# R read by rows, W and R loaded singly, more transposes by DMA, and a new hand-made order in a fused recurrence and feed-forward kernel

## The chip, the cores and the metric

The kernel runs on one core of one Trainium2 chip. The metric is the time of the device for one execution, in microseconds (us). A core has a matrix engine (PE in the profile, with its weight loads as PEld), a vector engine (DVE), a scalar or activation engine (ACT), a general one (POOL), a queue engine that here only issues transfers (SP), and 16 DMA engines that carry the transfers. Each engine works through its own list of instructions in the order in which the program holds it, and waits where an operand isn't ready.

## The reference, cut to what matters

Inputs r, k, v, w, a, b have the shape [4 batches, 8 heads, 768 tokens, 40]. The state of a head is a 40x40 matrix.

```python
for t in range(S):
    y[:, :, t] = np.einsum('bhd,bhde->bhe', rt, state)
    Sa = np.einsum('bhde,bhe->bhd', state, at)
    state_decay = state * wt[:, :, None, :] - np.einsum('bhd,bhe->bhde', Sa, bt)
    state = state_decay + np.einsum('bhd,bhe->bhde', vt, kt)

x = y.transpose(0, 2, 1, 3).reshape(3072, 320)     # one row per token
h = np.maximum(x @ w_in, 0.0)                      # 320 -> 2048
out = (h * h) @ w_out                              # 2048 -> 320
```

## The kernel before

**Tiling.** The 768 tokens are cut into 6 chunks of 128. One chunk of one batch entry is called a batch here, m = 0 to 23; m // 4 is the chunk. A batch holds 128 tokens (on the partitions) of 8 heads; each head's 40 columns are padded to 64, so that two heads make 128 columns. Inside a chunk the recurrence is done by matrix products and masks, and a state (UZ) goes from chunk to chunk. A batch is two steps, st = 2m and 2m + 1, of four heads each: 48 steps.

**Preparation of a batch** (add_prep). Six loads (W, K, B, A, V, R) on the SP queue. ln(W) on ACT, split into a high and a low part (hi, lo), summed along the tokens by PE (cs, L333), and turned into decays by ACT (GI and GA, L357, E). KB, AA, V and R are products or casts in bf16. Then they are turned, tokens to columns: KBT, AT, VT, RT. "Turned" means either PE transposes into a PSUM bank (turn, L417) with a copy out by DVE (L240) or ACT (L237), or one DMA transpose on the SP queue (across, L446). Before the change KB is turned by DMA from batch 8 on, and A, V and R always by PE. R of the first four batches is loaded "by rows" (L305, two transfers, runs of 1280 bytes, eight tokens to a partition) and turned by 16 transposes of 64x64 (L513), and by four of 128x128 (L417) after that.

**The last decay** GL of each batch, the last token's row of GA turned to a column: four products with one column on PE and a DVE product with a mask (L376, L381) in the first six batches; later one DMA transpose for two batches (gD, L385) and a POOL or DVE product with the mask.

**A step** (add_step): ca (PE, L563), its mask (CN, two of 128x512 on DVE, L571), P, two corrections, Sn; then tb, ex (PE, L641), its mask (EVX, two of 128x512 on DVE, L646), y (PE, L661 to L675), Xn (DVE, L681), and the carried state UZ. **The feed-forward** (add_ff) takes one batch at a time for the first four and two at a time later: the result Xn of two steps gets its last 64 columns doubled ("dup"), is turned by PE (tx, L816) and copied (XT), goes through w_in (hr, L841, and hp, L854), relu (hs), square (Gt) and w_out (op, L888), and is stored (L896).

**Loads.** From batch 4 on one transfer brings two batches (L297, 320 KB); each of the six tensors has three such buffers.

**Order.** Nothing is scheduled by the compiler. ORDER is a string of numbers, the one list in which all operations are emitted, and so each engine's own order; WAYS says which engine does an operation that several can do (a copy, a product); BANKS which PSUM bank a product uses; IDLE adds products without use (L1060) ahead of a PE operation. A transfer that waits on SP holds all transfers behind it. On PE, "R" operations (ca, ex, hr, and R's 64x64 transposes) use the array in row halves, "F" operations all of it.

Of the kernel before, what the change touches and what calls it, by code (L numbers as in the profile page):

```python
# [7 lines left out]
FP32 = mybir.dt.float32  # L8
# [11 lines left out]
def kernel(  # L20
# [39 lines left out]
    RING = {"N": 3, "NW": 2, "lnW": 2, "GI": 2, "KB": 5, "GA": 2, "E": 3, "AA": 2, "V": 5, "R": 3, "SN": 8,  # L60
            "EVX": 3, "RT": 4, "VT": 4, "KBT": 3, "AT": 3, "GL": 4, "GD": 2, "CN": 3, "c1": 2, "x1": 2,
# [3 lines left out]
    SPLIT, THREE, ROWS, GLD, PAIR = 1, 6, 4, 6, 4  # L65
# [116 lines left out]
    def blank(ring, i):  # L182
# [6 lines left out]
        if ring == "KB":  # L189
            nc.vector.memset(t_[:, :, :, D:64], 0.0)  # L190
        elif ring in ("AA", "V", "R"):
            nc.vector.memset(t_[:, :, D:64], 0.0)
        elif ring == "GA":
            nc.vector.memset(t_[:, :, :, D:64], 0.0)
        elif ring == "SN":
            nc.gpsimd.memset(t_[:, :, D:64], 0.0)
        elif ring == "UZ":
            nc.vector.memset(t_[:], 0.0)
# [7 lines left out]
    for i in range(2):  # L206
        blank("SN", i)
# [3 lines left out]
    for ring, a_, b_, eng, cost, lat, r0 in (  # L211
            ("KB", 1, RING["KB"], "DVE", 0.145, 0.22, -1.5), ("V", 1, RING["V"], "DVE", 0.09, 0.17, -1.2),
            ("R", 1, RING["R"], "DVE", 0.09, 0.17, -1.2),
            ("AA", 1, 2, "DVE", 0.09, 0.17, -1.5), ("GA", 1, 2, "DVE", 0.09, 0.17, -1.0),
            ("SN", 2, RING["SN"], "POOL", 0.1, 0.2, -1.5), ("HM", 0, 1, "POOL", 0.16, 0.26, 2.0),
            ("UZ", 0, 2, "DVE", 0.9, 1.0, 0.5)):
        for i in range(a_, b_):
            rank = i + r0 if ring != "UZ" else (7.0, 0.5)[i]
            later[ring, i] = ("blank", ring, i)
            op(("blank", ring, i), eng, rank, cost, lat, [], [],  # L220
               lambda ring=ring, i=i: blank(ring, i))
# [11 lines left out]
    BY_DMA = {"KB": range(8, NBC), "V": (), "A": ()}  # L233
# [23 lines left out]
    for m in range(NBC):  # L257
        o = Batch()
        bt.append(o)
        o.nat = bt[m - 1].nat if m % 2 else {key: buf(f"N{key}") for key in "WKBAVR"}  # L260
        o.lnW, o.hi, o.lo, o.GI, o.KB, o.AA, o.V, o.R, o.VT, o.RT, o.KBT, o.AT, o.GL, o.Xn = (
            buf(x) for x in ("lnW", "hi", "lo", "GI", "KB", "AA", "V", "R", "VT", "RT", "KBT", "AT", "GL", "Xn"))
        o.GA, o.E, o.GD = (bt[m - 1].GA, bt[m - 1].E, bt[m - 1].GD) if m % 2 else (buf(x) for x in ("GA", "E", "GD"))
# [20 lines left out]
    def add_load(m, key, rank):  # L284
        o = bt[m]
        c, bb = divmod(m, NB)

        def tile_():
            return sb(o.nat[key], [128, 2, NHH, D], FP32)
# [879 lines left out]
```

## Time and profile before

| what | value |
|---|---|
| median of 3 runs | 257.37 us (256.85 to 257.81) |
| the profiled execution's own time | 256.97 us |
| its span in the trace | 255.4 us |
| DMA: hardware queue, software queue | 76.5%, 6.2% of 16 engines' span |
| DMA packets | 172256, of which 165047 under 512 B |

The rows in the prediction come from the first page, from answers that group instructions ("line engine op out<-in xcount | busy, mean ns"), from windows of the span (busy time of each engine in a stretch), from the timeline (start, duration, engine, line), and from lists of waits. Matrix products overlap in the pipeline, and the ends that the profile shows for them are modelled: their pace is read from one start to the next.

### The profile page before, as it was taken

The page shows a single profiled execution, that of the slowest core. Times are in us where ns is not written, and L with a number is a line of the kernel's source. Part 1 is how long each engine was busy: PE and PEld are TensorE (multiplying, and loading weights), DVE is VectorE, ACT ScalarE, POOL GpSimd, SP SyncE. Part 2 cuts the span into 40 slices and gives each one's busy share as a digit, 9 for nine tenths or more (in the row PEclk, how much of TensorE's full clock was granted, in tenths as well). Part 3 has the DMA queues.
Part 4 walks back from the last instruction along what each step waited for, and adds up shares of the span by engine and source line. Part 5 has one row for each costly group of instructions (what it writes and reads, how often), then busy time and mean ns, then how long its engine had stood idle before and what let it go on. Part 6 is the DMA issues. An engine that isn't in the chain of part 4 may idle for free.

```text
span 255.4 us, 9993 instructions
## 1 busy us (share of the span) xinstructions
PE 242.0 (95%) x3948; PEld 193.1 (76%) x3948; DVE 230.4 (90%) x556; ACT 215.6 (84%) x589; POOL 172.0 (67%) x259
## 2 busy tenths in 40 slices
PE   7978889999999999999999999999999999999993
PEld 7656667787787687887788777877788787878772
DVE  6799999998799999999999999999998898999482
ACT  3669978898698898899999999998999798877660
POOL 4366784886696969875568979995748694716340
PEclk9999999999999999999999999999999999999999
DMA  6999999999599979889988899988898989300111
GB/s 111 189 176 149 174 217 177 147 153 215 101 150 192 168 134 181 173 153 165 200 159 165 160 190 173 167 176 156 154 168 123 214 188 152 70 30 5 68 35 68
DMA packets 172256, 37.95 MB, mean 149 GB/s; under 512 B 165047, under 2 KB 170679, under 8 KB 172206
## 3 DMA queue, kind: packets, MB, share of 16 engines
q1 hardware_dynamic: 169646, 34.66, 76.5%
q0 software_dynamic: 2560, 2.62, 6.2%
q8 instruction: 31, 0.51, 0.9%
q14 instruction: 19, 0.16, 0.2%
HBM read 28.84 MB, written 3.93 MB: 128 GB/s over the span
## 4 chain that ended last, share of the span: by engine, by line
PE 51%; ACT 2%; DVE 2%; DMA 2%; issue 1%; POOL 0%; SPq 0%; POOLq 0%; DVEq 0%
PE bank L888 16%; PE bank L854 10%; PE bank L417 4%; PE bank L641 3%; PE bank L841 3%; PE bank L563 3%; PE bank L595 2%; PE bank L661 2%; DMA NA<-in_a_dram 2%; PE bank L333 1%; PE bank L669 1%; PE bank L623 1%; PE bank L816 1%; PE bank L586 1%; PE bank L628 1%
## 5 line engine op out<-in xcount | busy, mean ns | idle before, releaser
L646 DVE TENSOR_TENSOR EVX<-bank,MEX 128x512 bf16<-128x512 f32 x96 | 62.4, 683 | 1.6 <-PE bank L641 1.1
L571 DVE TENSOR_TENSOR CN<-bank,MCN 128x512 bf16<-128x512 f32 x96 | 61.3, 682 | 1.9 <-PE bank L563 1.0
L888 PE MATMUL bank<-WOUT,Gt 128*128 128x320 bf16 x384 | 59.4, 300 | 0.4 <-DMA WOUT<-in_moe_w_out_dram 0.4
L872 POOL TENSOR_TENSOR Gt<-hs 128x512 bf16<-128x512 bf16 x43 | 45.2, 1055 | 19.2 <-ACT hs L861 14.0
L854 PE MATMUL bank<-XT,WIN 128*128 128x256 bf16 (+1 forms) x448 | 54.5, 258 | 0.0
L861 ACT ACTIVATE hs<-bank 128x512 bf16<-128x512 f32 x77 | 45.5, 601 | 6.0 <-issue 2.5
L888 PEld LDWEIGHTS <-Gt 128*128 128x128 bf16 x384 | 35.4, 97 | 13.3 <-issue 0.8
L854 PEld LDWEIGHTS <-WIN 128*128 128x128 bf16 x448 | 34.8, 97 | 7.1 <-issue 3.6
L612 ACT ACTIVATE junk<-CN 128x512 bf16<-128x512 bf16 x48 | 30.6, 638 | 0.2
L341 POOL TENSOR_TENSOR lo<-hi 128x320 f16<-128x320 f32 x21 | 15.1, 720 | 15.0 <-ACT hi L237 8.5
L401 POOL TENSOR_TENSOR KB<-NB,GI 128x320 bf16<-128x320 f32 (+1 forms) x22 | 18.7, 854 | 8.3 <-ACT GI L357 6.8
L870 ACT ACTIVATE Gt<-hs 128x512 bf16<-128x512 bf16 x37 | 23.1, 636 | 1.4 <-DVE hs L863 1.4
L595 PEld LDWEIGHTS <-CN 128*128 128x128 bf16 x384 | 18.5, 96 | 5.3 <-issue 2.6
L401 POOL TENSOR_TENSOR KB<-NK,GI 128x320 bf16<-128x320 f32 x21 | 18.6, 888 | 5.5 <-ACT GI L357 5.5
L407 POOL TENSOR_TENSOR AA<-NA,E 128x320 bf16<-128x320 f32 x19 | 15.3, 809 | 10.1 <-DMA NA<-in_a_dram 7.5
L563 PE MATMUL bank<-AT,KBT 64*128 64x128 bf16 x384 | 18.0, 218 | 2.2 <-ACT KBT L237 0.7
L841 PE MATMUL bank<-XT,WIN 64*128 64x256 bf16 (+1 forms) x224 | 18.5, 256 | 0.0
L661 PE MATMUL bank<-KB,EVX 128*128 128x40 bf16 x384 | 17.2, 180 | 0.0
L563 PEld LDWEIGHTS <-KBT 64*128 64x128 bf16 x384 | 12.2, 94 | 6.6 <-issue 2.8
L750 POOL TENSOR_TENSOR x<-Mc,c 128x640 bf16<-128x640 bf16 x10 | 14.0, 1398 | 3.9 <-PE bank L641 3.8
L237 ACT ACTIVATE SNall<-bank 128x160 bf16<-128x160 f32 x38 | 11.4, 307 | 6.0 <-PE bank L595 4.5
L681 DVE TENSOR_TENSOR Xn<-bank,E 128x160 bf16<-128x160 f32 x48 | 14.7, 316 | 1.8 <-PE bank L669 0.7
(134 smaller groups left out, 652.6 us busy)
## 6 DMA issues: line engine op xcount, KB each, us to landing
out_dram<-osb SPq DMA_DIRECT2D x24, 160.0 KB, 2.4
NW<-in_w_dram SPq DMA_DIRECT2D x10, 320.0 KB, 4.5
NK<-in_k_dram SPq DMA_DIRECT2D x10, 320.0 KB, 5.5
NB<-in_b_dram SPq DMA_DIRECT2D x10, 320.0 KB, 5.1
NA<-in_a_dram SPq DMA_DIRECT2D x10, 320.0 KB, 5.2
NV<-in_v_dram SPq DMA_DIRECT2D x10, 320.0 KB, 5.3
NR<-in_r_dram SPq DMA_DIRECT2D x10, 320.0 KB, 4.9
E<-GA SPq DMA_DIRECT2D x9, 224.0 KB, 4.6
```

The lines of the kernel that those rows point to most:

```text
L401: engine(eng).tensor_tensor(out=o.KB.tile[:, u, h, 0:D], in0=o.nat[key].tile[:, m % 2, h], op=ALU.mult, in1=o.GI.tile[:, h])
L563: nc.tensor.matmul(out=quads(ca[s])[:, i, u, :], lhsT=o.KBT.tile[half(s), u, j0 + i, :], rhs=o.AT.tile[half(s), j0 + i, :], start=(i == 0 ...
L571: nc.vector.tensor_tensor(out=t_[:, :, s], in0=quads(ca[s]), in1=MCN[:], op=ALU.mult)
L595: nc.tensor.matmul(out=P[:, 2 * i + s], lhsT=CN[:, i, s, 1, :], rhs=X[:, 2 * i + s], start=False, stop=last, skip_group_check=True)
L612: nc.scalar.activation(out=t_, in_=CN_.tile[:, :, :, 1, :], func=ACTF.Square, accum_out=ACC[:, AN + st:AN + st + 1])
L646: nc.vector.tensor_tensor(out=sb(EV_, [128, 2, 2, 2, L], BF16)[:, :, s], in0=quads(ex[s]), op=ALU.mult, in1=MEX[:].rearrange("p (i u) x -> ...
L841: nc.tensor.matmul(out=hv(w_)[:, u], lhsT=WIN[2][half(w_), j * 128:(j + 1) * 128], rhs=XT()[half(w_), 2, 0:nb, :], start=(u == 0), stop=False,
L854: nc.tensor.matmul(out=hv(w_)[:, u], lhsT=WIN[g][:, (j0 + u) * 128:(j0 + u + 1) * 128], rhs=XT()[:, g, 0:nb, :], start=False, stop=(g == 1 ...
L861: nc.scalar.activation(out=t_, in_=hpb.tile[:], func=ACTF.Relu)
L870: nc.scalar.activation(out=t_, in_=x_, func=ACTF.Square)
L872: engine(eng).tensor_tensor(out=t_, in0=x_, in1=x_, op=ALU.mult)
L888: nc.tensor.matmul(out=opb.tile[:, 0:DM], lhsT=Gtb[h].tile[:, j, b_, :], rhs=WOUT[:, j, :], start=(j == 0), stop=(j == NJ - 1))
```

## The change

1. R of every batch is loaded by rows (runs of 1280 bytes, two transfers) and turned on PE by 16 transposes of 64x64. Before this held for batches 0 to 3.
2. W and R are loaded one batch at a time, in rings of five single buffers (K, B, A and V still two batches at a time).
3. The last decay GL comes from PE products in all 24 batches, and its mask product is on DVE; the nine DMA transposes gD are gone.
4. x is turned by DMA from batch 12 on, V from batch 14 on and A from batch 20 on: 12 + 10 + 4 transfers of 384, 512 and 512 columns. Their PE transposes and copies out of PSUM are gone.
5. At the start, only the pad columns of UZ are set to zero (768 of 2048 elements), and each such clearing may be on DVE or POOL.
6. ORDER, WAYS and BANKS are new; IDLE holds 42 products in place of 84.

```diff
-    SPLIT, THREE, ROWS, GLD, PAIR = 1, 6, 4, 6, 4
+    SPLIT, THREE, PAIR = 1, 6, 4
...
+        if ring == "UZ":
+            t_ = t_[:].rearrange("p i (s d) -> p i s d", s=2)
+        fill.memset(t_[..., D:64], 0.0)
...
-    BY_DMA = {"KB": range(8, NBC), "V": (), "A": ()}
+    BY_DMA = {"KB": range(8, NBC), "V": range(14, NBC), "A": range(20, NBC), "X": range(12, NBC)}
...
-        o.nat = bt[m - 1].nat if m % 2 else {key: buf(f"N{key}") for key in "WKBAVR"}
+        o.nat = dict(bt[m - 1].nat) if m % 2 else {key: buf(f"N{key}") for key in "KBAV"}
+        o.nat.update({key: buf(f"N{key}") for key in "WR"})
...
         op(("L", m, key), "SP", rank, 0.6, 0.6, [], [o.nat[key]],
-           two if m >= PAIR else rows if key == "R" and m < ROWS else go)
+           rows if key == "R" else pair if two else go)
...
-        def gl_row():
-            nc.sync.dma_start_transpose(out=sb(o.GD, [128, 2 * PB, 32], BF16)[:],
-                                        in_=o.GA.tile[96:128].rearrange("p b h e -> p (b h e)"))
-        if m < GLD:
...
+        op(("gl", m), "PE", s0 - 0.5, *pe(0.102), [("GA", m), ("GI", m)], [o.GA, csb], gl_mm, "F")
+        op(("GL", m), "DVE", s0 - 0.3, 0.075, 0.16, [("gl", m)] + cleared("HM", 0), [csb, o.GL], gl_ev)
...
         def t_r():
-            if m >= ROWS:
-                turn(bank(b4), [flat(o.R.tile[:, 2 * j:2 * j + 2, :]) for j in range(PB)])
-                return
             for i in range(8):
...
+                def across_x(b_=b_, Xn_=Xn_):
+                    nc.sync.dma_start_transpose(out=XT()[:, :, b_, :], in_=Xn_.tile[:, 0:NG * 128])
...
+                op(("XT", h, b_), "SP", 2 * m + 6.0, 1.25, 1.25, [("Xn", 2 * m), ("dup", h, b_)], [Xn_, X_], across_x)
...
-    IDLE = ((135, 29, 7), (42, 8, 1), (44, 23, 2), (90, 10, 0), (329, 6, 0), (929, 8, 5),)
+    IDLE = ((32, 14, 7), (60, 5, 1), (56, 6, 2), (65, 7, 0), (145, 5, 3), (106, 5, 3),)
```

What the new order does at three places. The rows are the instructions of one engine in its order.

**DVE at the start**, before the first mask (CN). Before, from the fourth clearing of a pad on:

```order
L192 MEMSET V_104 128x8x12
L198 MEMSET UZ_110 128x1024
L192 MEMSET R_108 128x8x12
L194 MEMSET GA_96 128x16x12
L242 TENSOR_SCALAR hi_188<-lnW_178 128x320
L192 MEMSET AA_101 128x8x12
L240 CAST R_107<-NR_169 128x8x40
L192 MEMSET R_109 128x8x12
L242 TENSOR_SCALAR hi_195<-lnW_184 128x320
L190 MEMSET KB_91 128x16x12
L192 MEMSET V_105 128x8x12
L192 MEMSET V_103 128x8x12
```

And now, at the same place:

```order
L192 MEMSET V_106 128x8x12
L238 TENSOR_SCALAR hi_184<-lnW_180 128x320
L192 MEMSET SNall 128x4x12
L238 TENSOR_SCALAR hi_211<-lnW_207 128x320
L192 MEMSET R_108 128x8x12
L388 TENSOR_TENSOR KB_90<-NB_170,GI_224 128x4x40
L340 TENSOR_TENSOR lo_230<-hi_211 128x320
```

Most clearings, the cast of R and the first lo have gone to POOL, and hi follows one clearing of a small pad. POOL's list there, between its last mask and its first lo:

```order
L192 MEMSET SNall 128x4x24 x2
L192 MEMSET KB_92 128x16x24
L192 MEMSET SNall 128x4x24
L192 MEMSET GA_96 128x16x24
L192 MEMSET UZ_110 128x32x24
L340 TENSOR_TENSOR lo_189<-hi_184 128x320
```

Before, POOL had only three clearings of SNall there, and the first lo was on DVE.

**SP near batches 20 to 22** (L434 is the DMA transpose of KB, V and A in the changed file, L304 a load of R by rows, L297 one for two batches). Before:

```order
L367 DMA E_98<-GA_95 15x1024
L446 DMA_TRANSPOSE KBT_618<-KB_90 128x8x128
L297 DMA NV_485<-in_v_dram 128x16x40
L446 DMA_TRANSPOSE KBT_333<-KB_91 128x8x128
L896 DMA out_dram<-osb_1600 128x320
L896 DMA out_dram<-osb_1848 128x320
L297 DMA NR_573<-in_r_dram 128x16x40
```

And now:

```order
L887 DMA out_dram<-osb_1876 128x320
L292 DMA NW_325<-in_w_dram 128x8x40
L434 DMA_TRANSPOSE AT_581<-AA_100 128x4x128
L434 DMA_TRANSPOSE AT_279<-AA_101 128x4x128
L434 DMA_TRANSPOSE KBT_271<-KB_91 128x8x128
L434 DMA_TRANSPOSE VT_876<-V_106 128x4x128
L297 DMA NK_595<-in_k_dram 128x16x40
L434 DMA_TRANSPOSE VT_354<-V_102 128x4x128
L304 DMA NR_219<-in_r_dram 64x1x320 x2
```

Transposes of A and V have come in between, and every one of them waits for a product or cast on POOL, DVE or ACT, with the loads behind it.

**SP at the end.** Before, from the last transpose of KB on:

```order
L446 DMA_TRANSPOSE KBT_618<-KB_93 128x8x128
L896 DMA out_dram<-osb_1696 128x320
L896 DMA out_dram<-osb_1848 128x320 x2
L896 DMA out_dram<-osb_1600 128x320
L896 DMA out_dram<-osb_1696 128x320
L385 DMA_TRANSPOSE GD_2130<-GA_95 128x8x32
```

And now, from the same one on:

```order
L434 DMA_TRANSPOSE KBT_579<-KB_93 128x8x128
L796 DMA_TRANSPOSE XT_830<-Xn_623 128x3x128
L796 DMA_TRANSPOSE XT_830<-Xn_973 128x3x128
L887 DMA out_dram<-osb_1876 128x320
L887 DMA out_dram<-osb_1607 128x320
L887 DMA out_dram<-osb_1779 128x320
L434 DMA_TRANSPOSE VT_769<-V_104 128x4x128
L304 DMA NR_709<-in_r_dram 64x1x320 x2
L887 DMA out_dram<-osb_1876 128x320
L434 DMA_TRANSPOSE VT_876<-V_105 128x4x128
L887 DMA out_dram<-osb_1607 128x320
L796 DMA_TRANSPOSE XT_923<-Xn_878 128x3x128
```

The load of the last R now stands behind two transposes of x, three stores and a transpose of V, and x of the last two batches is turned here.

More of the change, by code (lines that the diff above doesn't have):

```diff
@@ L180, with blank @@
     )
-    def blank(ring, i):
+    def blank(ring, i, eng="DVE"):
+        fill = nc.gpsimd if eng == "POOL" else nc.vector
         if ring == "HM":
@@ L210 @@
     later = {}
[L211 to L216, printed above, removed]
+    for ring, a_, b_, n, r0 in (
+            ("KB", 1, RING["KB"], 384, -1.5), ("V", 1, RING["V"], 192, -1.2), ("R", 1, RING["R"], 192, -1.2),
+            ("AA", 1, 2, 192, -1.5), ("GA", 1, 2, 384, -1.0), ("SN", 2, RING["SN"], 96, -1.5),
+            ("HM", 0, 1, 0, 2.0), ("UZ", 0, 2, 384, 0.5)):
         for i in range(a_, b_):
@@ L305, in rows @@
                 nc.sync.dma_start(
-                    out=t_[64 * s:64 * s + 64].rearrange("p i e -> p (i e)"),
+                    out=tile_()[64 * s:64 * s + 64].rearrange("p i e -> p (i e)"),
                     in_=src.rearrange("(j s) (b i) e -> s b j (i e)", s=2, i=8)[s])
-        if m >= PAIR and m % 2:
+        if two and m % 2:
             alias["L", m, key] = "L", m - 1, key
```

201 lines of the change are left out of this document (95 added, 106 removed).

## The prediction

> **What bounds the kernel now.** I read the first page, then the span cut into stretches, then the chain of waits.
>
> ```profile
> PE 242.0 (95%) x3948; PEld 193.1 (76%) x3948; DVE 230.4 (90%) x556; ACT 215.6 (84%) x589; POOL 172.0 (67%) x259
> ```
>
> Three engines are nearly full, so a share of the whole span says little. The windows give the busy time of PE, PEld, DVE, ACT and POOL in each stretch (instructions in brackets), then the granted clock, the mean share of the DMA engines, and GB/s:
>
> ```profile
> 13.30:50.00 36.70, 31.54 (x613) 24.71 (x614) 35.45 (x89) 31.27 (x88) 24.03 (x38) 1.00 1.02 172
> 50.00:75.00 25.00, 23.48 (x431) 19.59 (x428) 21.92 (x52) 21.63 (x60) 20.01 (x27) 1.00 1.05 166
> 75.00:100.00 25.00, 24.58 (x417) 19.07 (x412) 24.64 (x57) 21.62 (x62) 20.11 (x28) 1.00 0.95 155
> 100.00:125.00 25.00, 24.91 (x418) 20.02 (x416) 24.28 (x60) 23.82 (x64) 16.60 (x24) 1.00 1.02 178
> 125.00:150.00 25.00, 24.96 (x422) 20.29 (x420) 23.87 (x61) 24.18 (x73) 21.33 (x32) 1.00 0.91 167
> 175.00:200.00 25.00, 25.00 (x417) 20.57 (x417) 22.87 (x54) 23.57 (x66) 16.35 (x26) 1.00 0.87 157
> 200.00:225.00 25.00, 24.79 (x397) 19.64 (x395) 23.05 (x56) 22.69 (x59) 15.68 (x26) 1.00 0.76 139
> ```
>
> Up to 50 us PE has gaps (5.2 of 36.7) while DVE is 97% busy and the DMA engines are full; from 75 to 125 DVE lacks only 1.1 us of 50; from 100 on PE shows no gap of note, and from 175 on DVE has 2 us free in each 25. The granted clock is 1.00 throughout. So I take **DVE (and the loads) as the limit up to about batch 12, and PE after it**. Late in the run one transfer still reaches the end's chain:
>
> ```profile
> 209.04 5.24 DMA NA<-in_a_dram
> POOL AA L407 <- DMA NA<-in_a_dram: 7.5, 3, 3.8
> ```
>
> The first row is a piece of the chain, the second a sum of waits (us, times, longest): one late load held POOL for 3.8 us.
>
> **Which batch stands where:** KBT goes by DMA for batches 8 to 23, and the rows of that line run from 80.3 to 216.9 us (quoted under SP below): 136.6 / 15 = 9.1 us a batch. Batch 12 is therefore near 117 us, 14 near 135, 20 near 190.
>
> **The change part by part, DVE and ACT.** Counting rows in the two orders, with the means of these groups (busy, mean ns):
>
> ```profile
> L240 DVE COPY AT<-bank 128x512 bf16<-128x512 bf16 (+1 forms) x16 | 6.5, 409 | 0.4 <-PE bank L417 0.4
> L240 DVE COPY VT<-bank 128x512 bf16<-128x512 bf16 (+1 forms) x13 | 5.2, 401 | 0.1
> L240 DVE COPY XT<-bank 128x384 bf16<-128x384 bf16 x12 | 4.0, 350 | 0.1
> L198 DVE MEMSET UZ<- 128x1024 uint32 x2 | 1.8, 912 | 0.3 <-issue 0.3
> L381 DVE TENSOR_TENSOR GL<-bank,HM 128x8 f32<-128x8 f32 x6 | 0.9, 156 | 0.0
> L237 ACT ACTIVATE XT<-bank 128x384 bf16<-128x384 bf16 x12 | 5.8, 491 | 0.9 <-PE bank L816 0.9
> ```
>
> DVE loses 7 copies of AT (2.9), 5 of VT (2.0), 6 of XT (2.1) and both full clearings of UZ (1.8), and gains 18 GL products from PSUM for 4 others, 14 x 0.156 = 2.2. That is 6.6 us less. ACT loses 6 copies of XT (2.9) and as many us of VT, and gives most of it back in other copies that WAYS moves to it. POOL takes casts and clearings, and it has 83 us free. Of the DVE relief, 1.8 us (UZ) and some small clearings fall at the start; much of the rest comes after batch 14, where PE is the limit.
>
> *Start.* Before:
>
> ```profile
> 4.03 0.47 ACT L323 ACTIVATE lnW<-NW 128x320 f32<-128x320 f32 x1 [1.71 <-DMA NW<-in_w_dram]
> 4.79 0.91 DVE L198 MEMSET UZ<- 128x1024 uint32 x1 [0.16 <-issue]
> 5.94 0.26 DVE L242 TENSOR_SCALAR hi<-lnW 128x320 f32<-128x320 f32 x1
> 7.11 0.81 DVE L341 TENSOR_TENSOR lo<-hi 128x320 f16<-128x320 f32 x2
> 10.59 0.53 POOL L401 TENSOR_TENSOR KB<-NB,GI 128x160 bf16<-128x160 f32 x1 [6.84 <-ACT GI L357]
> 13.29 2.48 DVE L571 TENSOR_TENSOR CN<-bank,MCN 128x512 bf16<-128x512 f32 x4
> ```
>
> ln ends at 4.50, but hi starts at 5.94, behind clearings, and lo only at 7.11 behind more of them and a cast. In the new order hi can end near 4.8; lo goes to POOL after five clearings. Their cost in this form isn't in the trace: at the least nothing, at the most the 0.91 us of the full UZ for each; I take about 0.3 each, near POOL's small fills, so lo starts near 5.1 instead of 7.11. That is 2 us, and I see nothing else on the path to the first mask that grows by as much: **-2.1** (range -2.5 to -0.5, the latter if clearings on POOL are slow).
>
> *From the first mask to batch 12.* DVE is 97% busy, so its relief shows if the loads keep up, which the DMA share of 1.02 makes doubtful. Leaving the start aside I count some 3.5 us less DVE work up to there (casts, relu and copies that move, UZ's second clearing of 0.91): at best -3.5, at worst 0; **-1.7**, the middle, since both limits stand in the same windows.
>
> *From batch 12 on, PE.* Starts of single groups:
>
> ```profile
> 222.19 0.39 PE L417 MATMUL bank<-IDb,R 128*128 128x128 bf16 x4
> 222.41 0.23 PE L580 MATMUL bank<-UZ,AT 128*128 128x80 bf16 x2
> 16.26 0.38 PE L417 MATMUL bank<-IDb,AA 128*128 128x128 bf16 x4
> 16.57 0.44 PE L513 MATMUL bank<-IDb,R 64*64 64x64 bf16 x16
> 16.94 0.29 PE L417 MATMUL bank<-IDb,V 128*128 128x128 bf16 x2
> 19.07 0.24 PE L376 MATMUL bank<-IDb,GA 128*128 128x1 bf16 x4
> 19.24 0.30 PE L333 MATMUL bank<-hi,UTS 128*128 128x320 bf16 x1
> ```
>
> Four transposes hold PE 0.22 us (222.19 to 222.41), R by rows 0.37 (16.57 to 16.94), the four products of the last decay 0.17. Gone: 14 groups of V and A, 14 x 0.22 = 3.1, and 12 of x with three each, 12 x 0.165 = 2.0. Added after batch 12: 11 x 0.15 = 1.6 for R and, by the place of these rows in the order, 10 x 0.17 = 1.7 for the last decay. Sum **-1.8**. (Over the whole kernel it is 20 x 0.15 + 18 x 0.17 - 5.1 = +1.0; the part ahead of batch 12 falls where PE has gaps. The 42 filler products that go also lay in such gaps.) With DVE and ACT behind each other at 92 to 97% here, their relief may add 2 us, and the DMA side may take it all: -4 to +2.
>
> The trace also shows an entry into R's block: 16.26 to 16.57 is 0.31 us for four transposes that take 0.22 otherwise, 0.09 more. On this the Trainium skill (TensorEngine Tiling (Array Packing), Key Properties) says that changing the tiling mode drains the engine, which the 0.09 us agrees with. By the rule all 20 new blocks pay, 20 x 0.09 = 1.8 us more, and the sum below would be 254.4 instead of 252.6. The new order sets nearly every R block beside ca, ex or hr, which change the mode anyway, so I leave it out.
>
> *End.*
>
> ```profile
> 237.19 0.23 PE L675 MATMUL bank<-TB,RT 128*128 128x80 bf16 x2
> 238.81 0.86 ACT L237 ACTIVATE XT<-bank 128x384 bf16<-128x384 bf16 x2
> 239.87 0.50 PE L841 MATMUL bank<-XT,WIN 64*128 64x256 bf16 x6
> L446 SPq DMA_TRANSPOSE KBT<-KB x16: 1231/1636/3578, 80.3 to 216.9; - x16
> DMA to landing us min/median/max: 3.0/4.1/5.6
> ```
>
> Before, 2.6 us lie between the last y (237.27) and the last feed-forward (239.87), filled by other products. Now x of the last batch goes by DMA: Xn and the doubling on DVE (about 0.7 with the step before it), then a transfer. KBT, 1024 columns, takes 3.0 us at the least; for 384 on an empty queue I take the same 3.0 (bounds 2 and 4.1). That makes 3.7 to 3.9, against 2.6 us of products that the new order puts after the last y. Behind the first hr on PE all the rest of the last feed-forward waits, and the stores on SP: **+1.2** (0 to +3).
>
> *Transfers.* DMA share in two stretches with little else:
>
> ```profile
> 218.20:222.00 3.80, 3.80 (x62) 3.04 (x57) 3.80 (x8) 3.71 (x10) 3.50 (x6) 1.00 0.48 111
> 224.00:230.00 6.00, 6.00 (x101) 4.70 (x98) 5.59 (x14) 4.45 (x13) 1.04 (x1) 1.00 0.09 31
> ```
>
> The first holds a KBT and a store, 0.48 x 3.8 = 1.8 us of all engines; the second one store, 0.54. So a KBT is near 1.3, half as much for A or V, 0.5 for x: 14 x 0.65 + 12 x 0.5 = 15 us added. R by rows has a store's shape (0.54 a batch); by pairs of short runs it is near 1.0 (the hardware queue's 76.5% of 255.4, less the transposes and stores, over 140 batch loads, gives 1.1): 20 x 0.5 = 10 us saved, early and late, and 9 gD go. The total changes by a few us at most; from 135 on it rises from a share near 0.9 to about 1.0. The single loads of W bring the same bytes. I put **0** for this, and keep its danger as rivals.
>
> **Sum:** 256.97 (own time of the profiled execution, 1.57 above its span) - 2.1 - 1.7 - 1.8 + 1.2 = 252.6. The median of the three runs is 0.4 above the profiled one: **253.0**.
>
> **Rivals.**
>
> *A. DVE is the limit nearly to the end.* For: above, 75 to 125. Against: 2 us free in each 25 from 175 on, and PE without a gap. Then PE's count doesn't matter and DVE's 6.6, plus what WAYS takes off it (Mc, casts, relu: some 7 us by count of rows), comes through for about two thirds, 9 us: 248.
>
> *B. The loads set the pace up to batch 12.* For: share 1.02 to 1.05 where PE has its gaps. Against: DVE is full there too. Then the first two terms vanish: 257.4 - 1.8 + 1.2 = 256.8, no change.
>
> *C. SP's single queue becomes the limit, and the kernel is slower.* From 125 to 215 us SP's own waits are:
>
> ```profile
> SPq L367 <- ACT hs L861: 3.6, 2, 1.9
> ...
> SPq L896 <- ACT TB L237: 0.3, 1, 0.3
> ```
>
> These are the first and last of 19 such rows, 33.9 us in sum, 3.4 a batch. The change adds for each batch from 14 on a V and an x transpose (1.23 us of issue at the least, 1.64 in the median) and some 1.2 us of issues for R and W, less half a gD: 2.5 us at the least, 3.4 at the median. At the minimum it fits; at the median nothing is left, and since each transpose waits in line for its product, loads come late. The point from which it decides is a mean issue of about 1.6 us. The price is that of the late NA, 3.8 us, twice more: 257.4 - 3.8 - 1.8 + 1.2 + 7.6 = 260.6. The last R, behind x, three stores and V, is the likeliest place.
>
> **Chances.** Forecast (250.5 to 256) 0.44; A 0.14; B 0.19; C 0.23. Within 0.5% (about what a measurement of this kernel can tell from no change) is 256.1 to 258.7: faster 0.59, same 0.18, slower 0.23. The range 247.5 to 260.5 takes in A and most of C.
>
> **What would show it.** First CN near 11.2 us instead of 13.3; DVE in 13 to 125 us still over 95%; PE without gaps from 100 us on; R's 16 transposes at 0.37 us; a gap of 1 to 1.5 us on PE ahead of the last hr; no wait of POOL or DVE for a load over 2 us after 125 us. The forecast is wrong if PE shows gaps after 125 us that end with a transposed AT, VT or XT or with NR, or if DVE falls under 90% while the time falls with it.

## The result, and the profile after

| | before | changed |
|---|---|---|
| median | 257.11 us (256.34 to 257.81) | **271.36 us** (268.91 to 272.94) |
| ratio to before, 95% interval | | **1.0523** (1.0413 to 1.0633): slower |
| the profiled execution, its span | 256.97, 255.4 us | 269.78, 268.3 us |

One of the changed kernel's four executions took 536.65 us, at full clock and for no reason that a trace shows; the range above and all ratios leave slow executions out and the medians don't, so that a difference of two medians, here and below, is good to about 1.5 us.

The change costs 13 to 14 us where 4 less were forecast, and the time lies above the forecast's range. These are the first page's rows of the changed kernel that answer to those of before: busy time of each engine, the granted clock and the DMA share in 40 slices of 6.7 us, the hardware queue, and the chain that ended last.

```profile
PE 242.7 (90%) x4126; PEld 192.6 (72%) x4126; DVE 223.3 (83%) x532; ACT 212.4 (79%) x579; POOL 180.6 (67%) x267
...
PEclk9899986999999999999999999999999799999998
DMA  6999989999789988879999987979869774852201
...
q1 hardware_dynamic: 162382, 37.09, 74.2%
...
PE 53%; DMA 16%; SPq 10%; ACT 7%; DVE 5%; POOL 5%; issue 3%; POOLq 0%; DVEq 0%; ACTq 0%
```

DVE and ACT lost the work that the prediction counted (DVE 230.4 to 223.3), and every engine stands idle longer, PE for 25.6 us where it was 13.4, POOL least (87.7 and 83.4). The chain tells for whom: before, 2% of it was DMA and 0% SP's issues, now 16% and 10%. So the kernel waits for transfers, though the hardware queue's packets take about as long in all as before (74.2% of 268.3 is 199 us of all engines; 76.5% of 255.4 was 195). The start of the recurrence in three batches says where the time went. The rows are DVE's from the timeline (start, duration, line): the first mask of the kernel and those of batches 12 and 23, changed kernel.

```profile
12.49 1.29 DVE L553 TENSOR_TENSOR CN<-bank,MCN 128x512 bf16<-128x512 f32 x2 [0.19 <-PE bank L545]
...
130.21 1.88 DVE L553 TENSOR_TENSOR CN<-bank,MCN 128x512 bf16<-128x512 f32 x3
...
238.02 1.28 DVE L553 TENSOR_TENSOR CN<-bank,MCN 128x512 bf16<-128x512 f32 x2
```

The same rows before (the first stands in the prediction, at 13.29):

```profile
124.32 1.28 DVE L571 TENSOR_TENSOR CN<-bank,MCN 128x512 bf16<-128x512 f32 x2
...
226.37 1.29 DVE L571 TENSOR_TENSOR CN<-bank,MCN 128x512 bf16<-128x512 f32 x2
```

The start gains 0.8, the way to batch 12 loses 6.7 (117.7 against 111.0), from there to batch 23 it is 5.8 more (107.8 against 102.0), and the end 1.2 more (30.3 against 29.0); rounding apart that is the 12.9 us between the spans. Two stretches of the changed kernel, with PE, PEld, DVE, ACT and POOL busy, the clock, DMA share and GB/s:

```profile
100.00:125.00 25.00, 21.48 (x387) 16.58 (x386) 19.55 (x49) 19.84 (x54) 17.71 (x26) 1.00 0.84 171
...
165.00:205.00 40.00, 36.38 (x614) 28.08 (x616) 34.72 (x80) 31.93 (x89) 28.29 (x39) 1.00 0.80 157
```

From 100 to 125 us PE was busy for 24.91 before and the DMA share was 1.02. Now PE waits at a clock of 1.00, and the engines' share has *fallen*. What PE, and POOL ahead of it, wait for stands in the list of waits (us in total, times, longest):

```profile
POOL KB L388 <- DMA NB<-in_b_dram: 5.3, 2, 3.6
...
PE bank L545 <- DMA AT<-AA: 2.3, 1, 2.3
```

The second row is one that the prediction named as a sign of being wrong: PE idle until a transposed AT has landed.

### The profile page after: what moved, and what is told of

The parts are those of the page before. It is cut to its first block, busy times and chain, and to the rows that moved or that the text cites. A ratio compares the mean times of both kernels' runs of the same rounds, so it can differ in the third digit from the quotient of the medians.

```text
span 268.3 us, 10437 instructions
## 1 busy us (share of the span) xinstructions
PE 242.7 (90%) x4126; PEld 192.6 (72%) x4126; DVE 223.3 (83%) x532; ACT 212.4 (79%) x579; POOL 180.6 (67%) x267
## 3 DMA queue, kind: packets, MB, share of 16 engines
q1 hardware_dynamic: 162382, 37.09, 74.2%
## 4 chain that ended last, share of the span: by engine, by line
PE 53%; DMA 16%; SPq 10%; ACT 7%; DVE 5%; POOL 5%; issue 3%; POOLq 0%; DVEq 0%; ACTq 0%
PE bank L879 13%; PE bank L845 10%; SPq L304 5%; DMA NB<-in_b_dram 4%; PE bank L545 4%; PE bank L832 4%; PE bank L623 3%; PE bank L405 3%; DMA E<-GA 3%; SPq L292 2%; PE bank L643 2%; PE bank L577 2%; PE bank L498 2%; DMA AT<-AA 2%; PE bank L332 2%
## 5 line engine op out<-in xcount | busy, mean ns | idle before, releaser
L863 POOL TENSOR_TENSOR Gt<-hs 128x512 bf16<-128x512 bf16 x43 | 44.5, 1043 | 30.8 <-ACT hs L852 30.0
L879 PE MATMUL bank<-WOUT,Gt 128*128 128x320 bf16 x384 | 60.0, 302 | 0.1
L852 ACT ACTIVATE hs<-bank 128x512 bf16<-128x512 f32 x80 | 46.5, 600 | 13.0 <-PE bank L845 9.6
L845 PEld LDWEIGHTS <-WIN 128*128 128x128 bf16 x448 | 35.4, 98 | 6.5 <-issue 2.3
L388 POOL TENSOR_TENSOR KB<-NB,GI 128x320 bf16<-128x320 f32 (+1 forms) x21 | 17.9, 857 | 7.9 <-DMA NB<-in_b_dram 5.3
L545 PE MATMUL bank<-AT,KBT 64*128 64x128 bf16 x384 | 19.0, 225 | 4.7 <-DMA AT<-AA 2.3
L861 ACT ACTIVATE Gt<-hs 128x512 bf16<-128x512 bf16 x35 | 22.1, 633 | 0.8 <-DVE hs L854 0.8
L388 POOL TENSOR_TENSOR KB<-NK,GI 128x320 bf16<-128x320 f32 x23 | 20.2, 882 | 1.1 <-ACT GI L356 1.1
L674 POOL TENSOR_TENSOR UZ<-us,GL 128x160 bf16<-128x160 f32 x29 | 13.2, 460 | 9.0 <-DVE us L668 8.9
L732 POOL TENSOR_TENSOR x<-Mc,c 128x640 bf16<-128x640 bf16 x12 | 16.8, 1396 | 1.0 <-ACT hs L852 0.9
```

What stands on the lines that cost most here:

```text
L388: engine(eng).tensor_tensor(out=o.KB.tile[:, u, h, 0:D], in0=o.nat[key].tile[:, m % 2, h], op=ALU.mult, in1=o.GI.tile[:, h])
L545: nc.tensor.matmul(out=quads(ca[s])[:, i, u, :], lhsT=o.KBT.tile[half(s), u, j0 + i, :], rhs=o.AT.tile[half(s), j0 + i, :], start=(i == 0 ...
L845: nc.tensor.matmul(out=hv(w_)[:, u], lhsT=WIN[g][:, (j0 + u) * 128:(j0 + u + 1) * 128], rhs=XT()[:, g, 0:nb, :], start=False, stop=(g == 1 ...
L852: nc.scalar.activation(out=t_, in_=hpb.tile[:], func=ACTF.Relu)
L863: engine(eng).tensor_tensor(out=t_, in0=x_, in1=x_, op=ALU.mult)
L879: nc.tensor.matmul(out=opb.tile[:, 0:DM], lhsT=Gtb[h].tile[:, j, b_, :], rhs=WOUT[:, j, :], start=(j == 0), stop=(j == NJ - 1))
```

## The experiments

Where nothing else is said, an edit keeps the order of the kernel that it starts from, as far as its operations are the same, and the ratio is to the kernel before, with its 95% interval.

### Is it the clock, or the order of the loads?

The page shows the clock at 0.6 to 0.8 of full speed in some slices. The first run puts 194 more filler products ahead of the six operations that end PE's longest gaps.

```diff
-    IDLE = ((32, 14, 7), (60, 5, 1), (56, 6, 2), (65, 7, 0), (145, 5, 3), (106, 5, 3),)
+    IDLE = ((32, 14, 0), (133, 33, 2), (60, 5, 1), (56, 6, 2), (65, 7, 5), (145, 5, 1), (413, 45, 2), (106, 5, 3), (890, 30, 4), (1459, 24, 6), (1561, 24, 2), (1799, 38, 2),)
```

> The changed kernel with 194 more products without use on PE, ahead of the six operations at which PE stood longest for an operand (gaps of 1.6 to 3.1 us at 7, 36, 122, 166, 200 and 206 us); nothing else moves. After such gaps the profile shows PE's granted clock at 0.5 to 0.8 for 5 us. Theory C (the low clock is a cost of its own): the clock returns to 0.99 or more and 4 to 7 us of the 14 come back, 264 to 267 us. Theory Q (SP's single line delivers late, the low clock only falls into time that is lost anyway): the clock returns as well, but the time stays within 2 us of 271. Theory O (the new order itself): no change.

**272.68 us, 1.057 (1.0489 to 1.065).** The late dips of the clock are gone (1.00 from 60 to 240 us, 0.99 without the fillers) and nothing is gained: PE waits behind the fillers for the same transfers. There the clock follows the gaps and isn't the cause. The early dips only moved (0.89 between 13 and 60 us, 0.92 without the fillers), so for them the run shows nothing.

The next run moves 75 loads on SP into the order in which they are needed (ORDER alone), and its sister does so with R by pairs, below.

> The changed kernel with the loads on SP in another order: at each place of SP's list where a load stood, the load stands that is needed first among those whose buffer is free (75 of the loads move; transposes, shifts, stores and all other engines stay). In the changed kernel R of batch 16 is issued at 108 us and used at 166, ahead of B of batch 12, issued at 111 and used at 115. Theory Q1 (loads that are not needed yet stand ahead of urgent ones): 4 to 8 us come back, 263 to 267. Theory Q2 (the number of issues and the waits in line count, not which load stands where): within 2 us of 271.

**269.66 us, 1.0463 (1.0419 to 1.0507)**: within the changed kernel's interval. The order of the loads among themselves isn't the cause.

### R by rows

Alone on the kernel before:

```diff
-    SPLIT, THREE, ROWS, GLD, PAIR = 1, 6, 4, 6, 4
+    SPLIT, THREE, ROWS, GLD, PAIR = 1, 6, 24, 6, 4
-           two if m >= PAIR else rows if key == "R" and m < ROWS else go)
+           rows if key == "R" else two if m >= PAIR else go)
```

> The kernel before with R of batches 4 to 23 loaded by rows and turned by 16 transposes of 64x64, nothing else: the four transfers of two batches stand where the one for both stood, in the same three buffers, and the order of everything else is the old one. Theory D: 20 batches hold the DMA engines for 1.2 us in place of 1.0, and the DMA engines are the limit to about 200 us: 258 to 263 us. Theory Q: 30 more issues of 0.6 us on a line that has some room here: 257 to 260. If rows save transfer time, as the prediction had it: 250 to 256.

**264.83 us, 1.0287 (1.0243 to 1.0332): 7.4 us slower**, more than any of the three theories gave. First SP's timeline, where R of two batches goes out, then three windows around it:

```profile
180.62 2.52 SPq L305 DMA_DIRECT2D NR<-in_r_dram  x4
```

```profile
178.00:181.90 3.90, 3.63 (x51) 2.54 (x50) 3.41 (x7) 3.23 (x9) 3.51 (x4) 1.00 0.74 136
182.00:185.90 3.90, 3.90 (x93) 3.49 (x91) 3.90 (x12) 3.79 (x10) 1.62 (x3) 1.00 0.48 138
186.00:190.00 4.00, 4.00 (x63) 2.92 (x60) 3.82 (x8) 4.00 (x14) 3.66 (x8) 1.00 0.92 161
```

The four transfers take 0.63 us each to issue, and while they and a store pass, the DMA engines are 0.48 busy at 138 GB/s; behind them the share is 0.92. So R by rows asks less of the engines (this kernel's queue share sank to 72.1% of 263.3 us, 190 us in place of 195) and the kernel is slower all the same. That it holds up the one queue is a reading that fits; the rows show the low share at one place and not what waited there. The reverse, on the changed kernel: R by pairs again, turned by four 128x128 transposes from batch 4 on.

```diff
-        two = m >= PAIR and key not in "WR"
+        two = m >= PAIR and key not in "W"
+            if m >= PAIR:
+                turn(bank(b4), [flat(o.R.tile[:, 2 * j:2 * j + 2, :]) for j in range(PB)])
```

> The changed kernel with R of batches 4 on loaded two batches at a time again (10 transfers in place of 40) and turned by four transposes of 128x128; V, A and x still by DMA. Theory Q in the form that R's rows crowd SP: SP loses 30 issues of 0.6 us and more, 18 us, and PE 3 us of transposes: 263 to 267. Theory Q in the form that the transposes and their waits in line are what holds the loads: within 2 us of 270. Theory O: within 2 us of 271.

**264.73 us, 1.0248 (1.0183 to 1.0313): 6.6 us better than the changed kernel**, as the first theory had it. With the loads in order of need as well:

> R by pairs as in e3 (264.7 us) and the loads by need as in e5. If the two causes add up: 258 to 261. If R's early loads were what stood ahead of urgent ones (so that e3 has removed it already): 263 to 266.

**265.57 us, 1.0312 (1.0255 to 1.037)**, the same again. Then the two halves of R's price. The data: in the next run, from batch 5 on each transfer of R brings 8 of its 64 rows, so most of R is stale.

```diff
-                    in_=src.rearrange("(j s) (b i) e -> s b j (i e)", s=2, i=8)[s])
+                    in_=src.rearrange("(j s) (b i) e -> s b j (i e)", s=2, i=8)[s, 0:nb])
```

> The changed kernel with R's loads by rows cut short: from batch 5 on each of the two transfers brings 8 of its 64 rows (what stands in the other rows of the buffer is that of an earlier batch, so part of R is left out); the issues on SP, their order, the 16 transposes and the copies stay. Theory D (the 16 DMA engines are the limit, and R by rows holds them longer than its packet time of 0.54 us a batch says): 19 batches lose some 1 us of transfer each, and the time falls to 250 to 258 us. Theory Q (SP's issues and waits in line, which stay): within 3 us of 271. PE's part of R by rows alone: no change.

**262.16 us, 1.0103 (1.006 to 1.0146): 9.2 us better with the same count of issues** (its executions spread from 258.75 to 265.50 us), between the ranges of the two theories. It also leaves out data that R by pairs would have to bring, so this isn't the price of reading by rows alone. The issues: R from batch 4 on leaves SP for POOL's software queue, same bytes.

```diff
-                nc.sync.dma_start(
+                (nc.gpsimd if m >= PAIR else nc.sync).dma_start(
```

> The changed kernel with R's loads by rows, from batch 4 on, issued by POOL on the software queue in place of SP: the same bytes and packets, 40 issues less on SP and 40 more on POOL. Theory Q in any form (SP's line): 262 to 267, unless POOL (67% busy) becomes the limit. If R's rows cost by PE's 16 small transposes and their copies instead: 270 or more.

**273.54 us, 1.0611 (1.0565 to 1.0658): nothing gained.** It isn't a clean test:

```profile
PE 244.6 (90%) x4126; PEld 192.9 (71%) x4126; DVE 231.1 (85%) x532; ACT 213.7 (78%) x579; POOL 199.7 (73%) x307
```

POOL spends 19 us on the issues, and DVE is busy for 7.8 us more with the same 532 instructions (3.9 more already with the loads by need, where POOL issues nothing of R). Shown is that R by rows costs some 7 us in either kernel, and that less data for the same transfers takes at least as much away. PE's 16 small transposes, which stay in that run, are thus at most a small part of it. Why the transfers cost what they do stays open.

### The transposes

The transposes of V, A and x alone, on the kernel before:

```diff
-    BY_DMA = {"KB": range(8, NBC), "V": (), "A": ()}
+    BY_DMA = {"KB": range(8, NBC), "V": range(14, NBC), "A": range(20, NBC), "X": range(12, NBC)}
```

> The kernel before with one part of the change alone: V from batch 14, A from 20, x from 12 turned by DMA, each transpose put about 1 us behind its product in the old order; R and W by pairs and the last decay by DMA stay. Theory Q: the 26 transposes in SP's line bring loads late also here: 260 to 267 us. Theory O (the new order is to blame, the transposes are harmless): 254 to 258.

**283.26 us, 1.1008 (1.0935 to 1.108): 26 us slower**, above the ranges of both theories, in an order that wasn't made for them. PE waits for XT there, 20.5 us in six waits. Do the consumers wait, or do the transfers cost? The next run leaves everything on PE as before and adds the same 26 transposes into a buffer (EX) that nobody reads.

```diff
+                    nc.sync.dma_start_transpose(out=sb(b_, [128, 4, 128], BF16)[:], in_=flat(x_.tile[:]))
```

> The kernel before with the 26 DMA transposes of V, A and x added into a buffer that nobody reads, about 1 us behind their products; PE turns V, A and x as before, so nothing waits for these transfers but SP's line and the DMA engines (one of nine buffers of TB gives its space). Theory D (transfer time): 18 to 22 us of transfers more from batch 14 on, of which some 10 find room: 263 to 270 us. Theory W (it is the wait for a transposed operand at PE that costs): 256 to 260.

**283.60 us, 1.1006 (1.096 to 1.1052).** Above both ranges again, and the same 26 us with nobody waiting for the result, so the wait at the consumers isn't needed for it. With a constant source, so that no transpose waits for a product:

```diff
-                    nc.sync.dma_start_transpose(out=sb(b_, [128, 4, 128], BF16)[:], in_=flat(x_.tile[:]))
+                    nc.sync.dma_start_transpose(out=sb(b_, [128, 4, 128], BF16)[:], in_=flat(MEX[:]))
```

> e10 with its 26 extra DMA transposes taken from a constant, and spread evenly over SP's list from batch 13 on: the same transfers, but they never wait for a product, so SP's line isn't held by them beyond the issue of 1.2 us each (31 us). Theory D (what transposes hold of the DMA engines, or of the issue): most of e10's 26 us stays, 268 to 280 us. Theory Q (SP stands still in front of a transfer whose product isn't ready, with the loads behind it): 257 to 262.

**281.81 us, 1.0959 (1.0907 to 1.1012).** Nor is it SP's wait for a product. The reverse, the same places and the same products to wait for, but a plain transfer of one row each:

```diff
-                    nc.sync.dma_start_transpose(out=sb(b_, [128, 4, 128], BF16)[:], in_=flat(x_.tile[:]))
+                    nc.sync.dma_start(out=flat(sb(b_, [128, 4, 128], BF16)[r0 + m:r0 + m + 1]), in_=flat(x_.tile[0:1]))
```

> e10 with each of the 26 extra transposes replaced by a plain transfer of one row (1 KB or less) of the same product at the same place of SP's list: the wait in line is the same, transfer time and issue are next to nothing (0.6 us each). Theory D: 257 to 262 us. Theory Q (waiting in line): most of e10's 26 us stays, 268 to 280.

**261.85 us, 1.0179 (1.0128 to 1.023).** The issues and the waits for products cost 4.4 us, the whole transposes 21.75 more. That isn't yet the price of transposing, for the two runs differ in one thing more: all added transposes write the one buffer EX, and SP holds each until the one before has landed, while the one-row transfers write a row each and never wait so. SP's waits with the whole transposes (us in total, times, longest), two of six such rows, 14.4 us in 12 waits together:

```profile
SPq L508 <- DMA EX<-Xn: 5.8, 3, 3.0
...
SPq L835 <- DMA EX<-Xn: 3.4, 3, 1.2
```

With the constant source it is 9.3 us in 7 waits. Nor is the loss spread over the transposes. Measured at the first mask of each batch, this kernel (283.60 us) is level with the one before up to batch 15 and falls back by 5.0 us at batch 16, 8.0 at 18 and 9.8 at 22, and hardly in between. SP's timeline ahead of the second of these:

```profile
177.63 1.34 SPq L508 DMA_TRANSPOSE EX<-V  x1
179.07 0.56 SPq L367 DMA_DIRECT2D E<-GA  x1
180.14 1.21 SPq L508 DMA_TRANSPOSE EX<-V  x1
181.40 0.59 SPq L297 DMA_DIRECT2D NA<-in_a_dram  x1
```

This load of A went out at 170.19 us with the one-row transfers. By 181.40 SP had waited for EX for 6.5 us in four waits, and from 180 to 184 us none of PE, DVE, ACT and POOL worked. So part of the 21.75 us is likely the one buffer's. The first run of this section has no such buffer and loses 26 us too, but with the waits at the consumers. What a transpose costs by itself these runs don't separate. Last, transposes of one block of 128 columns in place of four (three for x):

```diff
-                    nc.sync.dma_start_transpose(out=sb(b_, [128, 4, 128], BF16)[:], in_=flat(x_.tile[:]))
+                    nc.sync.dma_start_transpose(out=sb(b_, [128, 4, 128], BF16)[:, 0], in_=flat(x_.tile[:])[:, 0:128])
```

> The kernel before with the 26 additional transposes that nobody reads, at the same places and with the same waits as in the run with 283.60 us, but each over one block of 128 columns instead of 4 (3 for x): as many issues by SP, about 0.26 of the data. With one-row plain transfers there it was 261.85 us. Theory 1 (what counts is how long a transpose occupies the DMA engines): 261.85 + 0.26 x 21.75 = 267.5, so 264 to 271 us. Theory 2 (SP's issue of a transpose, 1.2 us against 0.6, is what counts, and it doesn't shrink with the data): 278 to 285 us.

**282.70 us; three executions took 282.55 to 283.10, one 277.76: about as much as the whole ones, up to some 5 us less.** My theory up to here, that their time on the DMA engines is the price, gave 264 to 271 us and falls. That a transpose costs the same at any size isn't shown by it: the wait for EX is here too, 18.2 us in 12 waits. SP's rows for EX (min, median, max in ns; whole, short, then plain transfers) and the windows from 130 to 205 us in the same three kernels:

```profile
L835 SPq DMA_TRANSPOSE EX<-Xn x12: 1179/1208/2285, 147.1 to 263.7; - x12
```

```profile
L835 SPq DMA_TRANSPOSE EX<-Xn x12: 1093/1108/2519, 147.7 to 264.3; - x12
```

```profile
L835 SPq DMA_DIRECT2D EX<-Xn x12: 497/528/2800, 146.1 to 243.8; - x12
```

```profile
130.00:205.00 75.00, 64.40 (x1007) 50.99 (x1006) 58.64 (x142) 59.28 (x170) 47.48 (x69) 0.91 0.82 154
```

```profile
130.00:205.00 75.00, 63.89 (x979) 50.12 (x976) 57.26 (x138) 57.23 (x164) 46.63 (x67) 0.89 0.73 139
```

```profile
130.00:205.00 75.00, 72.48 (x1195) 58.59 (x1193) 68.97 (x165) 68.89 (x196) 56.30 (x80) 1.00 0.84 159
```

A transpose takes 1.1 to 1.2 us to issue at the least, at either size, a plain transfer 0.5. With the short ones the engines' share is 0.73 in place of 0.82, and PE gets no more done (979 products against 1007): the engines have room, the kernel has none. The DMA engines' share in slices of 0.2 us, short transposes, from 153 us on, shows the room:

```profile
DMA  0000003300002898552038999999998500000899
```

The "33" is one short transpose. The engines are empty ahead of it, while SP waited for EX and then issued it, and for 0.8 us behind it, until the next transfer, issued at 154.36 us, begins. Behind a second short one there is a hole of 1 us again, ahead of the transpose of KB that SP issues from 159.18 to 160.44.

On the changed kernel the transposes of V, A and x go back to PE (BY_DMA as before, but its other parts and its order kept):

> The changed kernel with V, A and x turned by PE again in all batches (26 DMA transposes go; their PE transposes and copies out of PSUM stand at the same places of the order), all the rest as changed. Theory Q: SP loses 26 transposes of 1.2 us and more and their waits in line, so loads after batch 11 come in time: 6 to 10 us come back, 261 to 265 us. Theory C: the late gaps go with the transposes (122, 166, 200, 206 us), the early ones stay: 265 to 267. Theory O, or R's loads alone to blame: within 2 us of 271, or worse by the 5 us of work that DVE, ACT and PE take up again.

**278.18 us, 1.073 (1.064 to 1.0821): 6.8 us slower than with them**, where the theory that they hold up the loads gave 261 to 265, and the one that blames the order or R up to 5 us more than the changed kernel. The two intervals just miss each other. So within the new order the transposes are no cost; the reading is that PE, DVE and ACT need the relief there more than the queue needs the room.

### Is SP's stream of issues the limit?

By the traces SP's issues take 195.6 us in sum before and 228.4 in the changed kernel, where SP is in an issue for 92 to 95% of each stretch from 60 to 240 us. (The expectations below have the sums at 206.7 and 242.7 us, and the stores in them at 32.6 and 29.7; by the traces these are 22.1 and 17.6.) Two runs have ACT issue the 24 stores, on its own queue:

```diff
-                nc.sync.dma_start(out=out[tok:tok + L, :], in_=osbb.tile[:])
+                nc.scalar.dma_start(out=out[tok:tok + L, :], in_=osbb.tile[:])
```

> The changed kernel with its 24 stores of the output issued by ACT instead of SP, at the same places of the order; the bytes, the transposes, R by rows and everything else stay. SP spends 29.7 of its 242.7 us in these issues. Theory 1 (SP's one queue is the limit: a transfer holds it for its issue or for its data, whichever is longer, and the DMA engines stand empty for about a microsecond behind a small transpose): some 25 us leave the queue before 240 us, and by what the added issues cost in the runs with 264.83, 261.85 and 282.70 us, 0.2 to 0.55 of that shows: 5 to 14 us less, 257 to 266 us, and the DMA share between 60 and 200 us rises. Theory 2 (the DMA engines' occupancy is the limit): the same transfers, 269 to 274 us. ACT gets 24 issues of at least 0.45 us, 11 us on 212, which costs either theory up to 5 us if they stand in its way.

**267.03 us, 1.038 (1.0321 to 1.0439)**: 4.3 us below the changed kernel, between the ranges of the two theories, and the two intervals overlap, so the gain isn't secured.

> The kernel before with its 24 stores issued by ACT instead of SP, nothing else. SP spends 32.6 of its 206.7 us in them. Theory 1 (SP's one queue is the limit here too): 0.2 to 0.55 of some 25 us, less ACT's cost, 248 to 256 us, which would beat both kernels. Theory 2 (the DMA engines' occupancy): 257 to 262 us.

**258.34 us, 1.0043 (1.0014 to 1.0071): nothing gained**, as the second theory had it. SP's issues summed to 208.9 us in the first of these, 19.5 less, for some 4 us of time. By these two runs a full SP is not a limit by itself; a reading, not tested, is that it waits with the transfers in its queue.

### Does less for the queue make it faster?

Three runs on the kernel before, each with an order fitted anew by the same procedure, on durations taken from these traces. The control has the new order alone:

> The kernel before with the same operations and only another order, fitted in the same way as that of the run with less work by DMA. It is the control for that run. Theory 1: the transfers are the same, so a new order can win little, 252 to 258 us. Theory 2: the order is what is worth something, so this run gains as much as the one with less work by DMA, 240 to 250 us.

**273.94 us, 1.0619 (1.0548 to 1.069).** Neither theory: this fitted order costs 16 us, with the same operations. With the last decays by products (9 transposes fewer):

```diff
-        if m < GLD:
+        if True:
```

> The kernel before with the last decays of all batches by products, as the change has it (the 9 transposes GD<-GA go, 18 small PE products with their DVE copies come), and an order fitted to it; nothing else of the change. Theory 1: 9 transposes of about 1 us fewer, 246 to 253 us. Theory 2: the products cost PE and DVE as much as they did, 256 to 260 us.

**267.99 us, 1.0445 (1.0385 to 1.0506).** And with KB turned by DMA from batch 12 only, and E spread by PE and ACT up to batch 11:

```diff
-    SPLIT, THREE, ROWS, GLD, PAIR = 1, 6, 4, 6, 4
+    SPLIT, THREE, ROWS, GLD, PAIR = 1, 12, 4, 6, 4
-    BY_DMA = {"KB": range(8, NBC), "V": (), "A": ()}
+    BY_DMA = {"KB": range(12, NBC), "V": (), "A": ()}
```

> The kernel before with less work for the DMA engines: the last decays of all batches by products (the 9 transposes GD<-GA go), KB turned by DMA from batch 12 instead of 8 (4 transposes fewer, their 16 turns a batch by PE and the evictions by DVE or ACT), the decays of batches 6 to 11 spread by PE and ACT instead of by DMA (no E<-GA for them), and an order fitted to that. R, V, A, x and all loads as before. Theory 1 (the DMA engines are full up to about batch 20, and what they are asked for sets the pace): 13 transposes of about 1 us and 3 pairs of E<-GA fewer, so 238 to 249 us. Theory 2 (the pace is set by PE, DVE, ACT and POOL and by the order in which they stand, and the DMA engines only look full): the engines get more work, 257 to 264 us.

**262.88 us, 1.0215 (1.0169 to 1.0262).** All three missed what the first theory gave them, only the last fell into the second's range, and none beats the kernel before. Against the control the steps go the expected way, 6 us for 9 transposes and 11 us for 13 transposes and the E of three pairs of batches, but three orders, each fitted apart, are thin ground for a price.

## Why the prediction was wrong, step by step

- **The step that failed is "Transfers: 0".** It priced R by rows at a store's 0.54 and so "10 us saved", the 26 transposes at 15 us of all engines, and let the two cancel. Both terms were counted in the engines' time. The runs show R by rows at +7.4 alone and +6.6 within the change, although the engines' time did fall, by 5 to 6 us (195 to 190), half of what was counted. So the engines' time isn't what sets its price. The first mask's delay shows the same inside the change: with R by pairs the loss up to batch 12 is 3.9 in place of 6.7 us, and from there to batch 23 it is 3.0 in place of 5.8. The transposes have no single price: 26 us in the order of before, where one buffer or waiting consumers may be part of it, and a gain of 6.8 in the new order. How R holds up the rest is argued at most: its four transfers keep SP for 4 x 0.63 us at half the engines' use, but R on POOL's queue gained nothing, as far as that test goes. A mean share near 1.0 was read as engines that are full; the changed kernel is slower at a share of 0.80 to 0.84.
- **What bounds the kernel:** "PE after batch 12" held for before only. In the changed kernel PE has gaps from 100 to 125 us and from 165 on, and DVE is at 78% from 100 to 125 us where "over 95%" was to be seen.
- **Start, -2.1:** measured -0.8. The prediction had hi end near 4.8 us; it starts at 5.54, behind DVE's mask MCN, which took 1.87 us where it took 0.47 before. POOL's new row of clearings runs without a pause from 3.34 to 5.15 us beside it, the last 0.73 us long; that they held up MCN is likely and not tested. Then the second lo stayed on DVE, 0.81 us at 8.71, so PE waits 1.89 us for it at 9.58. MCN before, then the changed kernel:

```profile
3.42 0.47 DVE L204 TENSOR_SCALAR MCN<-MEX 128x256 bf16<-128x256 bf16 x2 [0.93 <-POOL MEX L177]
```

```profile
3.42 1.87 DVE L198 TENSOR_SCALAR MCN<-MEX 128x256 bf16<-128x256 bf16 x2 [0.93 <-POOL MEX L177]
...
4.42 0.73 POOL L192 MEMSET UZ<- 128x768 bf16 x1
...
8.71 0.81 DVE L340 TENSOR_TENSOR lo<-hi 128x320 f16<-128x320 f32 x1
...
9.58 0.30 PE L332 MATMUL bank<-lo,UTS 128*128 128x320 f16 x1 [1.89 <-DVE lo L340]
```

- **First mask to batch 12, -1.7:** +6.7. The relief of DVE and ACT is there, but this stretch already waited for loads, as the term itself doubted, and R by rows falls into it (2.8 of the 6.7).
- **From batch 12 on, -1.8:** +5.8. The work that goes off DVE goes, and waits for transfers take its place.
- **End, +1.2:** +1.2 measured, by luck. The gap of 1 to 1.5 us on PE ahead of the last hr isn't there: other products fill the time until 252.72 us, the last transpose of x lands at 252.79, 2.3 us behind its issue where 3.0 were taken, and hr starts at 252.84. From the last y to the last hr it is 2.9 us in place of 2.6. The other 1.0 lies ahead of the last y, 11.9 us behind batch 23's first mask where it was 10.9.
- **42 fillers that go, clock 1.00:** the clock does sink to 0.92 in 13 to 60 us. Fillers at the late gaps gained nothing; those at the early ones didn't bring the clock back, so what it costs there isn't known.
- **Rivals.** C had the sign, and two late loads of 3.8 us for its price, 7.6 us where by its own sum some 18 came. Its ground was a mean issue of 1.6 us; by the trace the new transposes' mean is 1.49, below that point, and the kernel is slower all the same. R's and W's issues, which it put at "some 1.2 us" more a batch, took 73 us in sum in place of 30, some 2.1 more for each of the 20 batches. B named the loads as the limit up to batch 12, but asked only what that hides, not what R by rows adds to it.
- **The mode change in R's blocks** (0.09 us) needed no price: with the blocks kept and R's data cut, 9.2 us came back, so R's blocks aren't where most of the time goes.

The sum that the runs bear: R by rows +6.6, about half of what the change costs. The rest of the change without it is at 264.73, 7.6 above the kernel before, and no run splits that. The transposes of V, A and x aren't it, since without them the changed kernel is slower still. The new order is the rival that was left: another order with the same operations cost 16 us, and this one was never run with the old operations.

**What stays open:** the cause of those 7.6 us, with the new order's own share, and why R by rows costs what it does. Open too is what a small transpose costs by itself: the same runs with a buffer for each added transpose would tell.

On R the Trainium skill (DMA: Bandwidth & Descriptors, Specifications) gives 512 bytes as the least transfer for line rate. By that rule the change from runs of 160 to 1280 bytes should win. In the engines' time it did (190 us in place of 195), in the kernel's it lost 7.4 us, and the measurement decides. Each transfer had also become four times smaller, 80 KB in place of 320; whether that is the reason wasn't tested.

## What to carry to other kernels

Price a transfer by what it costs in a run, not by its share of 16 engines: R by rows left the engines half empty while it went out, took less of their time in all, and still cost 7 us. Before work is moved off a busy engine to a queue whose loads already end the busy engine's waits, add the same transfers with nobody reading them to the old kernel, each into a buffer of its own, or they wait for one another as they did here. What they cost holds for that order only: the transposes that cost 26 us in the old order were worth 6.8 in the new one. And look where a loss falls: most of the 26 us with nobody reading came in three stops, not as 26 small prices.

## What had not been expected of the hardware

- A DMA transpose of 128 columns is hardly cheaper to issue than one of 384 or 512: 1.11 against 1.21 us in the median, and 26 of them in one buffer cost about as much run time (282.70 and 283.60 us).
- DVE's first mask product, MCN, took 1.87 us in place of 0.47 while POOL cleared buffers without a pause. It was so in the changed kernel and in four more runs with its order, and wasn't tested alone.
- With R's issues on POOL's software queue DVE's 532 instructions took 231.1 us in place of 223.3; with another order of the loads alone they took 227.2.
- Taking 24 issues off a full SP frees next to nothing, though ACT issues a store in some 0.34 us: -4.3 us at best in one kernel and +1.1 in the other.
